# RWKV attention with a soft mixture of experts on one core: w, k and r laid channel-major by the host, decay scans over whole rows

## The chip, the core and the metric

The kernel runs on one core of a Trainium2 chip. The metric is the device time of one execution in microseconds (us). Of three runs of the kernel before, the fastest took 243.7, the slowest 246.23, and the median is 245.06 us. The traces come from a profiled execution of the same program. Engines are named as in the profile: PE (TensorE matmuls, PEld their weight loads), DVE (VectorE), ACT (ScalarE), POOL (GpSimd), SP (SyncE, which here only issues DMAs).

## The reference

Two parts follow each other. First a recurrent attention over B=4 batches, H=8 heads, S=768 tokens and D=48 channels, with a state matrix of 48x48 for each head that decays by w in every token:

```
for t in range(S):
    kt, vt, rt, wt = (k[:, :, t], v[:, :, t], r[:, :, t], w[:, :, t])
    cur = einsum('bhd,bhe->bhde', u[None] * kt, vt)
    y[:, :, t] = einsum('bhd,bhde->bhe', rt, state + cur)
    state = wt[:, :, :, None] * state + einsum('bhd,bhe->bhde', kt, vt)
```

Then x = y as 3072 tokens of 384 numbers goes through a soft mixture of 8 experts with 4 slots each: logits = x @ phi (32 columns), a softmax over all tokens gives what each slot takes in, each expert computes relu(slot @ w1) @ w2 with a hidden size of 1024, and a softmax over the 32 slots mixes the results into each token. The experts' weights are 25 MB, and all of it is float32.

## The kernel before

**Pairs and chunks.** The 32 combinations of batch and head are handled as 16 pairs of heads, and the 768 tokens of a pair as C=6 chunks of 128. In a pair's tiles the first head's 48 channels stand in rows 0 to 47 and the second's in rows 64 to 111, so these tiles have 112 rows; rows 48 to 63 are filler. For each chunk the recurrence is written as products: with G the decay from a token to the chunk's end and Rc the decay from the chunk's start divided by the decay of the whole chunk, K times G and R times Rc give the scores of every two tokens of a chunk by one matmul, and a state at each chunk's start is carried on by one short scan.

**One pass** of the loop over `it` (17 passes) works on two pairs at once, and on the logits of an older one:

- Stage A on pair `it`. w, k and r are loaded with tokens in rows. PE turns them, 128x112 at a time, with the identity as operand (`a_wT` L200, `a_turn` L235, 18 transposes). DVE scans w backward for G (`a_back` L212, one scan a chunk) and forward for Rc (`a_fwd` L221, one scan a chunk, out of PSUM both), and scales the turned k and r out of PSUM into `KTt` and `RTt` (`a_scale` L241). ACT copies the decays of whole chunks into `pat` and checks the range of the decays (`a_pat` L247, L249, `a_check` L205). POOL multiplies r, k and u (`d_rk` L254, `d_rku` L260) and DVE sums the product to `a` (`d_a` L265), the factor with which a token's own v enters.
- Stages B and C on pair `n = it-1`. PE turns five chunks of the scaled k back (`b_kn` L279, copied by ACT in L281), makes the scores in two halves of three chunks and two heads (`b_scores` L292; ACT copies two 128x384 tiles a half out of PSUM in L296 and POOL masks them in L297), and the 48x48 updates of the state (`b_u` L313). DVE scans the state over the chunks, a head at a time (`b_state` L321). PE then sums scores times v (`c_av` L335) and r times state (`c_inter` L348: one matmul with 112 rows for both heads, since `Sb` holds the two heads' states as a block diagonal), and DVE adds a·v (`av` is made by POOL, L270) and writes x, half a pair at a time (`c_evac` L357).
- In three of four passes from the fourth on (X), the logits of 128 columns of x: six transposes (`l_turn` L366, copied by ACT in L368), three matmuls with phi (`l_mm` L383), a copy (L388). In every fourth pass (Y: 6, 10, 14) the softmax of a finished batch, and in the pass behind it (Z: 7, 11) its slots.

**After the loop** come the rest of the softmax, the two projections of the experts (`hp` L515, `so` L549) and the mixing (`op` L593), with the output stored in 14 pieces.

**What sets the order.** The order is written by hand: each engine runs its instructions in the order of the program text, and waits at the head of its queue for what the next one needs. All loads and stores are issued by SP in that order too. The weights are loaded in thirds of a tile, `PER_IT[it]` thirds in a pass; what is left goes out after the loop.

## Time and profile before

| | us |
|---|---|
| runs: fastest, median, slowest | 243.7, 245.06, 246.23 |
| profiled execution: span | 244.0 |
| start, up to the first kn transposes of pass 3 | 34.55 |
| passes 3 to 15 | 147.70 |
| after that: pass 16, end of the softmax, experts, mixing | 61.75 |

The profiled execution's own time isn't listed apart from its span; the median of the runs lies 1.06 us above that span. The three stages are read from the chain of waits, in which every pass from the third on begins with the five transposes of L279.

In the rows of the prediction, the chain of waits gives start, duration and the engine, result and line of each piece of the chain that ended last. A group's row gives the line, engine, operation, result and source with their sizes, how often it ran, then its busy time in all, the mean duration of one in ns, and the idle time before it with what ended it. A timeline row begins with start and duration. The rows of stretches give the stretch, its length, the busy time of PE, PEld, DVE, ACT and POOL with the number of instructions, then the clock granted to PE as a share of full speed, the share of time for which the DMA engines were busy, and GB/s.

### The profile page before, as it was taken

The page shows a single profiled execution, that of the slowest core. Times are in us where ns is not written, and L with a number is a line of the kernel's source. Part 1 is how long each engine was busy: PE and PEld are TensorE (multiplying, and loading weights), DVE is VectorE, ACT ScalarE, POOL GpSimd, SP SyncE. Part 2 cuts the span into 40 slices and gives each one's busy share as a digit, 9 for nine tenths or more (in the row PEclk, how much of TensorE's full clock was granted, in tenths as well). Part 3 has the DMA queues.
Part 4 walks back from the last instruction along what each step waited for, and adds up shares of the span by engine and source line. Part 5 has one row for each costly group of instructions (what it writes and reads, how often), then busy time and mean ns, then how long its engine had stood idle before and what let it go on. Part 6 is the DMA issues. An engine that isn't in the chain of part 4 may idle for free.

```text
span 244.0 us, 7186 instructions
## 1 busy us (share of the span) xinstructions
PE 211.9 (87%) x2824; PEld 158.8 (65%) x2824; DVE 183.7 (75%) x464; ACT 97.2 (40%) x265; POOL 106.6 (44%) x156
## 2 busy tenths in 40 slices
PE   7759798989898899989798989897989999979850
PEld 3448586868677667768596768687768652346650
DVE  4997969798989888899979798999793744203540
ACT  0623436445262616372544354353536531203330
POOL 5346478465472828382737274563725131000000
PEclk9997979999997999999979999997999999999975
DMA  4988958939795969698696959994959278994994
GB/s 93 181 171 150 178 104 180 199 107 185 223 225 156 230 164 271 119 249 162 207 173 206 179 185 180 309 233 185 288 177 313 68 248 273 318 326 145 334 309 120
DMA packets 122072, 49.54 MB, mean 203 GB/s; under 512 B 101424, under 2 KB 118960, under 8 KB 122032
## 3 DMA queue, kind: packets, MB, share of 16 engines
q1 hardware_dynamic: 122032, 49.02, 79.2%
q8 instruction: 24, 0.39, 0.7%
q14 instruction: 16, 0.13, 0.2%
HBM read 44.29 MB, written 4.72 MB: 201 GB/s over the span
## 4 chain that ended last, share of the span: by engine, by line
PE 44%; DVE 38%; issue 6%; DMA 5%; SPq 2%; ACT 1%; POOL 1%; DVEq 0%; POOLq 0%; ACTq 0%
DVE Rc L221 13%; PE yp L348 13%; DVE G L212 12%; PE yp L335 6%; DVE Sb L321 6%; DVE KTt L241 5%; DMA wt<-in_moe_w_dram 4%; PE wt L200 4%; PE tp L279 4%; PE so L549 3%; PE hp L515 3%; PE op L593 3%; SPq L173 2%; PE sp L428 2%; PE tp L235 2%
## 5 line engine op out<-in xcount | busy, mean ns | idle before, releaser
L270 POOL TENSOR_TENSOR av<-vt,a 128x576 f32<-128x576 f32 x16 | 18.6, 1162 | 60.0 <-DVE x L357 38.9
L235 PE MATMUL tp<-ident,wrk 128*112 128x128 f32 x192 | 32.1, 299 | 13.8 <-DVE KTt L241 13.1
L212 DVE TENSOR_TENSOR_SCAN G<-wt,floor 112x128 f32<-112x128 f32 x96 | 32.0, 401 | 9.9 <-PE wt L200 9.6
L221 DVE TENSOR_TENSOR_SCAN Rc<-wt,Rc,ceil 112x127 f32<-112x127 f32 x96 | 37.6, 459 | 0.6
L348 PE MATMUL yp<-Sb,RTt 112*64 112x96 f32 x320 | 33.7, 353 | 3.8 <-DVE Sb L321 3.3
L235 PEld LDWEIGHTS tp<-ident,wrk 128*112 128x112 f32 x192 | 20.6, 140 | 24.2 <-DVE KTt L241 17.7
L297 POOL TENSOR_SCALAR_AFFINE_SELECT at<-at 128x384 f32<-128x384 f32 x64 | 31.8, 520 | 10.3 <-ACT at L296 10.2
L296 ACT COPY at<-ap 128x384 f32<-128x384 f32 x64 | 27.6, 482 | 20.6 <-PE ap L292 19.8
L281 ACT COPY kn<-tp 128x336 f32<-128x336 f32 (+1 forms) x32 | 11.0, 397 | 56.2 <-PE tp L279 56.2
L335 PEld LDWEIGHTS yp<-vt,at 128*64 128x64 f32 x768 | 29.0, 150 | 3.9 <-issue 1.6
L292 PE MATMUL ap<-RTt,KTt 48*128 48x128 f32 x384 | 30.9, 289 | 0.0
L335 PE MATMUL yp<-vt,at 128*64 128x48 f32 x768 | 30.8, 234 | 0.0
L292 PEld LDWEIGHTS ap<-RTt,KTt 48*128 48x128 f32 x384 | 24.8, 187 | 5.7 <-issue 4.7
L348 PEld LDWEIGHTS yp<-Sb,RTt 112*64 112x64 f32 x320 | 22.3, 157 | 7.2 <-DVE Sb L321 6.1
L254 POOL TENSOR_TENSOR rk<-wrk 128x576 f32<-128x576 f32 x16 | 22.6, 1414 | 9.4 <-ACT rk L205 8.7
L321 DVE TENSOR_TENSOR_SCAN Sb<-up,pat 48x288 f32<-48x288 f32 x32 | 24.0, 749 | 2.1 <-PE up L313 1.9
L260 POOL TENSOR_TENSOR rk<-rk,u_bc 128x576 f32<-128x576 f32 x16 | 22.5, 1405 | 1.9 <-DMA u_bc<-in_u_dram 1.7
L357 DVE TENSOR_TENSOR x<-yp,av 128x288 f32<-128x288 f32 x32 | 14.5, 454 | 7.8 <-PE yp L348 7.7
L241 DVE TENSOR_TENSOR RTt<-tp,Rc 112x384 f32<-112x384 f32 x32 | 16.5, 553 | 2.2 <-PE tp L235 1.8
L241 DVE TENSOR_TENSOR KTt<-tp,G 112x384 f32<-112x384 f32 x32 | 16.0, 538 | 0.0
L200 PE MATMUL wt<-ident,wrk 128*112 128x128 f32 x96 | 14.0, 282 | 1.3 <-POOL rk L254 0.7
L205 ACT ACTIVATE rk<-wrk,b_low 128x576 f32<-128x576 f32 x16 | 12.6, 786 | 6.5 <-DVE a L265 6.5
(125 smaller groups left out, 280.0 us busy)
## 6 DMA issues: line engine op xcount, KB each, us to landing
wt<-in_moe_w_dram SPq DMA_DIRECT2D x24, 512.0 KB, 4.9
wt<-in_moe_w_dram SPq DMA_DIRECT2D x4, 1536.0 KB, 6.9
vt<-in_v_dram SPq DMA_DIRECT2D x16, 288.0 KB, 4.0
wrk<-in_w_dram SPq DMA_DIRECT2D x30, 144.0 KB, 2.9
wrk<-in_k_dram SPq DMA_DIRECT2D x30, 144.0 KB, 3.4
wrk<-in_r_dram SPq DMA_DIRECT2D x30, 144.0 KB, 3.9
wt<-in_moe_w_dram SPq DMA_DIRECT2D x5, 576.0 KB, 8.2
wt<-in_moe_w_dram SPq DMA_DIRECT2D x3, 960.0 KB, 8.5
```

The costliest lines, as they stand in the source:

```text
L200: nc.tensor.transpose(out=wt[0:PITCH, c // 3, (c % 3) * P:(c % 3 + 1) * P], in_=win(st["t"], W_OFF, c), identity=ident)
L212: nc.vector.tensor_tensor_scan(out=G[0:PITCH, c, 0:P][:, ::-1], data0=wc[:, ::-1], data1=floor[0:PITCH].broadcast_to([PITCH, P]), initial= ...
L221: nc.vector.tensor_tensor_scan(out=Rc[0:PITCH, c, 1:P], data0=wc[:, 0:P - 1], data1=ceil[0:PITCH].broadcast_to([PITCH, P - 1]), initial=Rc ...
L235: nc.tensor.transpose(out=tp[0:PITCH, j, :], in_=win(st["t"], off, 3 * hf + j), identity=ident)
L241: nc.vector.tensor_tensor(out=st[which][0:PITCH, cs, :], in0=st[which, hf][0:PITCH], in1=fac[0:PITCH, cs, :], op=ALU.mult)
L254: nc.gpsimd.tensor_tensor(out=rk, in0=chd(st["t"], R_OFF), in1=chd(st["t"], K_OFF), op=ALU.mult)
L292: nc.tensor.matmul(out=aps[h][:, cc, :], lhsT=st["KT"][rows, c, :], rhs=st["RT"][rows, c, :], start=True, stop=True)
L296: nc.scalar.copy(out=at, in_=aps[h])
L297: nc.gpsimd.affine_select(out=at, in_=at, pattern=[[0, 3], [1, P]], compare_op=ALU.is_gt, fill=0.0, base=0, channel_multiplier=-1)
L321: nc.vector.tensor_tensor_scan(out=Sb[rows, h * D:(h + 1) * D, :].rearrange("p e n -> p (e n)"), data0=st["up"][rows].rearrange("p e n -> ...
L335: nc.tensor.matmul(out=yp[cols, cc, h, :], lhsT=st["AT", h, hf][:, cc, cols], rhs=st["vv"][:, h, 3 * hf + cc, :], start=first[th], stop=False)
L348: nc.tensor.matmul(out=st["yp", hf][cols, cc], lhsT=st["RT"][0:PITCH, c, cols], rhs=Sb[0:PITCH, :, c], start=False, stop=(cc == 2))
```

## The change

- The host hands over w, k and r of a pair as one array `wkr`: channels in rows, and in a row first 774 numbers of w (6 chunks of 128, with a 0 between them), then 768 of k and 768 of r. A pass loads it with two DMAs of 48 rows (`a_load`) into one of three rotating tiles `ld0`, `ld1`, `ld2`. v, phi, u, w1 and w2 are laid out by the host in the order of the tiles too, so that each row of a load is one piece; w2's columns are stored in the two parts (240 and 144) in which they are loaded at the end. The output is written as two arrays of 240 and 144 columns, which the host joins.
- The 18 transposes of w, k and r are gone. G is one backward scan over 774 numbers (`a_back` L177); the decay forward is one scan in place over w's own 774 (`a_fwd` L184), with the reciprocals of the chunks' decays put in at each chunk's start. k and r are scaled in place, each by one 112x768 multiplication (`a_scale` L190).
- `a` is made on PE: r times k, with channels in rows, is one POOL multiplication of 112x768 (`d_rk` L208), and six matmuls multiply it by u and sum over the channels (`d_a` L214), copied by ACT (L217). POOL's product with u and DVE's sum are gone.
- The state of both heads is one scan of 112x288 (`b_state` L264), no longer a block diagonal. r times state is therefore a matmul for each head (`c_inter` L293: 20 a pass with 48 rows, before 10 with 112).
- The result of a pair is one PSUM tile of two banks, evacuated by one instruction (`c_evac` L303).
- The order within a pass is another, the scores have three PSUM banks where they had two, and two thirds of a weight tile are loaded in each pass from 2 on.

The core of the diff:

```diff
+    def a_load(i, first=False):
+        t = lds[i % 3]
+        for lo, hi in ((0, K_OFF), (K_OFF, LOAD)) if first else ((0, LOAD),):
+            for h in range(2):
+                nc.sync.dma_start(out=t[64 * h:64 * h + D, lo:hi], in_=wkr[i, h, :, lo:hi])
...
+    def a_back(i):
+        t = lds[i % 3]
+        nc.vector.tensor_tensor_scan(
+            out=G[0:ROWS][:, ::-1], data0=t[0:ROWS, 1:SCAN + 1][:, ::-1], data1=g_base[0:ROWS][:, ::-1],
+            initial=1.0, op0=ALU.mult, op1=ALU.max)
+
+    def a_fwd(i):
+        t = lds[i % 3]
+        nc.vector.reciprocal(out=by_chunk(r_base)[:, :, 0], in_=by_chunk(G)[:, :, 0])
+        nc.vector.tensor_tensor_scan(
+            out=t[0:ROWS, 0:SCAN], data0=t[0:ROWS, 0:SCAN], data1=r_base[0:ROWS],
+            initial=1.0, op0=ALU.mult, op1=ALU.max)
+
+    def a_scale(i, off, fac, lo):
+        w_ = win(lds[i % 3], off)
+        nc.vector.tensor_tensor(out=w_, in0=w_, in1=by_chunk(fac)[:, :, lo:lo + P], op=ALU.mult)
...
     def d_a(i):
-        st = sts[i]
-        st["a"] = a = small.tile([P, C, 2, 1], F32, name="a")
-        nc.vector.tensor_reduce(out=a, in_=rk, axis=AX.X, op=ALU.add)
+        ap = ps_t.tile([P, C, 2], F32, name="aps", tag="tp")
+        for c in range(C):
+            nc.tensor.matmul(out=ap[:, c, :], lhsT=rk[0:ROWS, c * P:(c + 1) * P], rhs=u_sb[:, i % NG, :],
+                             start=True, stop=True)
+        sts[i]["a"] = a = small.tile([P, 2, C, 1], F32, name="a")
+        nc.scalar.copy(out=a.rearrange("p h c o -> p c (h o)"), in_=ap)
...
             for th in range(2):
                 cols = slice(64 * th, 64 * th + 64)
-                nc.tensor.matmul(
-                    out=st["yp", hf][cols, cc], lhsT=st["RT"][0:PITCH, c, cols], rhs=Sb[0:PITCH, :, c],
-                    start=False, stop=(cc == 2))
+                for h in range(2):
+                    rows = slice(64 * h, 64 * h + D)
+                    nc.tensor.matmul(
+                        out=st["y"][cols, h, c * D:(c + 1) * D],
+                        lhsT=t[rows, R_OFF + c * P + 64 * th:R_OFF + c * P + 64 * th + 64],
+                        rhs=Sb[rows, :, c], start=False, stop=(c == C - 1))
```

The order of a pass, as the program now has it (shortened to the attention and the logits):

```
        if B_:
            d_av(n)
        if A:
            a_back(it)
        if B_:
            b_kn(n)
            b_scores(n, 0)
        if A:
            d_a(it)
            a_scale(it, K_OFF, G, 1)
        if B_:
            b_u(n)
            b_state(n)
            b_scores(n, 1)
        if A:
            a_pat(it)
            a_fwd(it)
        if X:
            xT = l_turn(xb[mb], mg - 1, once, ps_t)
            ...
            l_part(mg - 1, xT, lts[mb], ps_t)
        if A:
            a_scale(it, R_OFF, lds[it % 3][:, 0:SCAN], 0)
        if B_:
            c_y(n)
            c_av(n, 0)
            c_inter(n, 0)
        ...
        if it + 1 < NIT:
            d_rk(it + 1)
            a_check(it + 1)
        if B_:
            c_av(n, 1)
            c_inter(n, 1)
            c_evac(n)
```

The PE queue in an X pass (pass 8), before: `wt` and `tp` from `wrk` are the transposes of w, k and r, `tp` from `x` those for the logits, `ap` the scores, `up` the state's updates, `lp` the logits, and `yp` the two products that sum to the attention's result.

```order
L279 MATMUL tp<-ident,KTt 128x112 x5
L200 MATMUL wt<-ident,wrk 112x128 x6
L366 MATMUL tp<-ident,x 128x128 x6
L292 MATMUL ap<-RTt,KTt 128x128 x6
L313 MATMUL up<-vt,kn 48x48 x10
L383 MATMUL lp<-xT,phi_sb 32x256 x3
L235 MATMUL tp<-ident,wrk 112x128 x6
L292 MATMUL ap<-RTt,KTt 128x128 x6
L235 MATMUL tp<-ident,wrk 112x128 x6
L335 MATMUL yp<-vt,at 64x48 x12
L348 MATMUL yp<-Sb,RTt 64x96 x4
L335 MATMUL yp<-vt,at 64x48 x12
```

Six matmuls of scores and ten of updates stood between the transposes of x and the logits made of them. The same pass on PE after, where `ld_101` is the pair's tile (k in the first place and r in the second of each score, k in the transposes) and `aps` the new product with u:

```order
L231 MATMUL tp<-ident,ld_101 128x112 x5
L242 MATMUL ap<-ld_101 128x128 x6
L214 MATMUL aps<-u_sb,rk 128x2 x6
L258 MATMUL up<-vt,kn 48x48 x10
L242 MATMUL ap<-ld_101 128x128 x6
L312 MATMUL tp<-ident,x 128x128 x6
L329 MATMUL lp<-xT,phi_sb 32x256 x3
L278 MATMUL y<-vt,at 64x48 x12
L293 MATMUL y<-Sb,ld_101 64x48 x8
L278 MATMUL y<-vt,at 64x48 x12
L293 MATMUL y<-Sb,ld_101 64x48 x12
```

The logits now stand directly behind the transposes that they need, and both halves of the scores ahead of them. The ACT queue of pass 8 before, where `kn`, `xT`, `at` and `lt` are copies out of PSUM, and L205 and L249 the checks:

```order
L281 COPY kn<-tp 128x336
L281 COPY kn<-tp 128x224
L205 ACTIVATE rk,chk<-wrk,b_low 128x576
L368 COPY xT<-tp 128x384 x2
L296 COPY at<-ap 128x384 x2
L388 COPY lt_1313<-lp 96x256
L296 COPY at<-ap 128x384 x2
```

The copies `xT` stood ahead of both pairs of score copies. The same queue after:

```order
L232 COPY kn<-tp 128x336
L232 COPY kn<-tp 128x224
L246 COPY at<-ap 128x384 x2
L217 COPY a<-aps 128x6x2
L246 COPY at<-ap 128x384 x2
L201 COPY pat_138<-G 112x48x5
L203 ACTIVATE junk_1232,chk<-G,b_one 112x6
L314 COPY xT<-tp 128x384 x2
L334 COPY lt_1093<-lp 96x256
L195 ACTIVATE xT,chk<-ld_100,b_low 112x768
```

The copies `xT` now stand behind both pairs of score copies, the copy of `a`, `pat` and one check.

More of the change, by code (lines that the diff above doesn't have):

```diff
@@ L75, in rwkv_soft_moe @@
     r32 = const.tile([P, NS], F32, name="r32")
[L76 to L77 removed]
     other = const.tile([TG, NTG, NS], F32, name="other")
[L79 to L83 removed]
+    u_sb = const.tile([ROWS, NG, 2], F32, name="u_sb")
     phi_sb = const.tile([P, KT, NS], F32, name="phi_sb")
@@ L225, in a_alloc @@
-    def a_alloc(i):
-        st = sts[i]
-        st["KT"] = kr.tile([P, C, P], F32, name="KTt")
-        st["RT"] = kr.tile([P, C, P], F32, name="RTt")
-    def a_turn(i, which, hf):
-        st = sts[i]
-        st[which, hf] = tp = ps_t.tile([P, 3, P], F32, name="tp")
-        off = K_OFF if which == "KT" else R_OFF
-        for j in range(3):
-            nc.tensor.transpose(out=tp[0:PITCH, j, :], in_=win(st["t"], off, 3 * hf + j), identity=ident)
-    def a_scale(i, which, hf):
-        st = sts[i]
-        fac = G[:, :, 1:P + 1] if which == "KT" else Rc
-        cs = slice(3 * hf, 3 * hf + 3)
-        nc.vector.tensor_tensor(out=st[which][0:PITCH, cs, :], in0=st[which, hf][0:PITCH],
-                                in1=fac[0:PITCH, cs, :], op=ALU.mult)
+        nc.sync.dma_start(out=vt, in_=v[i])
@@ L581, in mix @@
         wd = hi - lo
-        out_v = out.rearrange("(t p) d -> p t d", p=P)
+        out_v = (out_a, out_b)[half]
         sends, t = {}, 0
```

578 lines of the change are left out of this document (228 added, 350 removed).

## The prediction

> **What bounds the kernel now.** I read the chain of waits first, since engines with a high busy share can still be waiting for each other in turn. Pass 10 of the loop, and the marks of the stages:
>
> ```profile
> 6.64 2.37 DMA wrk<-in_r_dram
> ...
> 34.55 0.63 PE tp L279 x5
> ...
> 74.07 1.38 PE tp L235 x6
> ...
> 102.57 0.63 PE tp L279 x5
> 103.19 0.67 PE wt L200 x6
> 103.96 2.00 DVE G L212 x6
> 106.21 1.28 DVE Rc L221 x4
> 107.73 0.83 DVE Rc L221 x2
> 108.56 0.91 DVE KTt L241 x2
> 110.14 0.77 DVE Sb L321
> 110.96 0.89 PE yp L348 x8
> 111.84 0.69 PE yp L335 x24
> 112.53 1.03 PE yp L348 x12
> ...
> 182.25 0.63 PE tp L279 x5
> ...
> 207.81 9.86 DMA wt<-in_moe_w_dram
> ```
>
> A pass is a ring: PE turns k and w, DVE scans, scales and scans the state, PE finishes, and the next pass's transposes begin at 112.53+1.03=113.56, 11.0 us after 102.57. Some 6.4 us of it, from 103.96 to 110.91, is DVE work for which PE's last products wait. Neither engine is full, and both are on the path. Thirteen passes take 182.25-34.55=147.7 us (11.36 each, the passes with softmax work included); the start takes 34.55, the rest 244.0-182.25=61.75, of which 9.86 is a wait for the experts' weights.
>
> **The DVE half of the ring.** Groups of instructions by line, with the mean duration in ns of one:
>
> ```profile
> L212 DVE TENSOR_TENSOR_SCAN G<-wt,floor 112x128 f32<-112x128 f32 x96 | 32.0, 401 | 9.9 <-PE wt L200 9.6
> L321 DVE TENSOR_TENSOR_SCAN Sb<-up,pat 48x288 f32<-48x288 f32 x32 | 24.0, 749 | 2.1 <-PE up L313 1.9
> L241 DVE TENSOR_TENSOR RTt<-tp,Rc 112x384 f32<-112x384 f32 x32 | 16.5, 553 | 2.2 <-PE tp L235 1.8
> L270 POOL TENSOR_TENSOR av<-vt,a 128x576 f32<-128x576 f32 x16 | 18.6, 1162 | 60.0 <-DVE x L357 38.9
> L254 POOL TENSOR_TENSOR rk<-wrk 128x576 f32<-128x576 f32 x16 | 22.6, 1414 | 9.4 <-ACT rk L205 8.7
> L297 POOL TENSOR_SCALAR_AFFINE_SELECT at<-at 128x384 f32<-128x384 f32 x64 | 31.8, 520 | 10.3 <-ACT at L296 10.2
> ```
>
> A scan costs 401 ns for 128 and 749 for 288 numbers a row, so 2.2 ns a number and 0.12 us for itself: one over 774 is an estimated 1.8 us by that slope and 2.4 by L212's mean alone (401x774/128). I take 1.8, since the fixed part is paid once, and two are 3.6 where twelve now take 2.00+1.28+0.83 and gaps. K and R scaled in one piece of 768 each are at most twice 0.553, and with two fixed parts saved about 0.92. The state's two scans become one of 0.77. A DVE pass is then 1.8+0.92+0.77+0.2 (reciprocals)+1.8+0.92+0.75 (one eviction of 576, between 0.55 and 0.92 by L241) = 7.1 us, some 0.9 more on average for the softmax. No link to PE is left between these steps except the state scan, since no transpose feeds the scans and scalings any more. POOL loses the product with u: 1.16 (L270) + 4x0.52 + 1.9 (r times k, 1.41 taken from 576 to 768 numbers) = 5.1 us. Both are below what follows for PE, DVE even at 2.4 a scan.
>
> **The PE half.** The timeline of PE, then that of ACT, where the clock is full:
>
> ```profile
> 113.50 0.70 PE L279 MATMUL tp<-ident,KTt 112*128 112x112 f32 x5
> 114.03 0.82 PE L200 MATMUL wt<-ident,wrk 128*112 128x128 f32 x6
> 114.78 0.94 PE L292 MATMUL ap<-RTt,KTt 48*128 48x128 f32 x12
> 115.65 0.66 PE L313 MATMUL up<-vt,kn 128*48 128x48 f32 x20
> 116.24 0.87 PE L235 MATMUL tp<-ident,wrk 128*112 128x128 f32 x6
> 117.03 0.94 PE L292 MATMUL ap<-RTt,KTt 48*128 48x128 f32 x12
> ```
>
> ```profile
> 118.06 0.86 ACT L296 COPY at<-ap 128x384 f32<-128x384 f32 x2 [0.77 <-PE ap L292]
> 118.80 0.62 ACT L247 COPY pat<-G 112x240 f32<-112x240 f32 x1
> 119.32 0.31 ACT L249 ACTIVATE junk<-G,b_one 112x6 f32<-112x6 f32 x1
> 119.52 0.19 ACT L249 ACTIVATION_READ_ACCUMULATOR junk<-G,b_one 112x1 f32 x1
> ```
>
> Matmuls overlap at their ends, so I price them from start to start: kn 0.53, a half of scores 0.87 (115.65-114.78), the updates 0.59, six transposes 0.79. The change takes 18 transposes (3x0.79=2.4) from PE and adds two things that the trace does not show. The product with u is 12 matmul records (six, each in two parts) with 128-wide weights and two columns; by the 20 narrow records of L313 it would be 0.36, by the transposes at 0.13 each 1.58; I take 0.87, as for the scores, whose weight loads are alike. r times state becomes 40 records with 48 columns where it was 20 with 96: between 0.029 each as in L335 (0.69/24), so 1.17, and the 0.89+1.03=1.92 of today; I take 1.17, since records of L335 have the same columns and their price has not to do with rows. The X pass in PE's new order:
>
> - kn 0.53, scores 0.87, product with u 0.87, updates 0.59, scores 0.87: issued by 3.73. The transposes of x end at 4.52.
> - ACT can copy the second scores from 2.86+1.0=3.86 on (118.06-117.03=1.0 from their start to the copies). Behind them stand pat (0.74 after them), the check (0.52) and its accumulator, 0.39 together from 119.32 on, so the copies xT begin at 5.51, and with two copies of the L296 kind and a handover (0.92) the logits start at 6.43. All else on PE is queued behind them: it stands 1.9 us.
> - logits 0.56 (three matmuls with 256 columns, estimated between 0.39 and 0.79), scores times v 0.70 twice, r times state 1.17: 9.5 us.
>
> So PE has 7.6 us of work and waits 1.9 in ten of the thirteen passes; DVE with 7.1 to 8 fits in, with the eviction last and 2 us of room. Two more prices, the slots from the chain of waits and the softmax's exponential from the instructions of its tile:
>
> ```profile
> 88.28 1.42 PE sp L428 x12
> ```
>
> ```profile
> L410 ACT ACTIVATE dT<-lt,nM x1: 514/514/514, 116.5 to 116.5; 96x256 f32<-96x256 f32 x1
> ```
>
> A Y pass has no logits, but transposes of that exponential, which ACT gives out behind the same check: 5.51 plus 0.51 and 0.19 for its sum, 0.4 for four narrow transposes and 2.57 for the products, about 9.2. Passes 7 and 11 add the slots, 10.9. ACT has about 6.2 us of copies a pass, POOL 5.1: both hidden by PE's 9.5; if PE fell below 8, DVE would be late next. The sum: 8x9.5+3x9.2+2x10.9=125.4, against 147.7.
>
> **The clock.** The last price is of the 1.9 us wait. Three stretches, and PE's clock as granted in them:
>
> ```profile
> 50.38:53.79 3.41, 2.58 (x42) 2.01 (x42) 3.40 (x8) 1.67 (x5) 2.31 (x4) 1.00 0.05 17
> ...
> 70.86:74.27 3.41, 2.18 (x41) 1.76 (x40) 3.34 (x10) 1.91 (x7) 3.41 (x6) 1.00 0.98 314
> 74.27:77.69 3.42, 3.42 (x38) 3.06 (x36) 3.34 (x8) 0.64 (x2) 0.40 (x2) 0.50 0.34 79
> ```
>
> After 3.41 us in which PE was busy for 2.18, the next 3.42 us were granted half the clock; after 2.58 they weren't. So 0.9 to 1.2 us of idle time in such a window suffices. A wait of 1.9 us leaves that much in one window unless it is split near its middle: I count a drop in 9 of 10 passes. A drop showed as 1.38 for six transposes (74.07) where 0.79 is usual, so 3.4 us at half clock do the work of some 2.0. That costs 1.4 where PE is the bound throughout, and nothing where DVE is late anyway; I take 1.2, since after the wait PE has 3.1 us of work without another wait. Thirteen passes: 13x0.9x1.2=14, and the loop is 139.5, so 8.2 us less than before.
>
> The Trainium skill, in "TensorE: Matmul & The Clock Gate", section "HAM oscillation — how this bites in real kernels", puts the rule as PE gaps of over about 3.4 us. By it a wait of 1.9 would cost no clock and the loop would be 125.4. The rows differ: a window with 1.23 us idle in all was followed by half clock, so the sum goes by the rows, and the rule's result is rival B.
>
> **Start, end and loads.** The first pass now waits for eleven issues and a landing at 6.64+2.37=9.0; four DMAs of w, k and r come first in the new order, so scans start at an estimated 6.5 (4.5 to 7). Pass 0's scans and scalings, with POOL's 1.9 for r times k ahead of k's scaling, end near 12.2; pass 1 with PE at half clock near 20.4; pass 2 on DVE's bound of 7.7 near 28.1. That is 6.5 less than 34.55. The end keeps its matmuls. Its transfers get longer rows. The page's GB/s in 40 slices, and a stretch of the loop's end:
>
> ```profile
> GB/s 93 181 171 150 178 104 180 199 107 185 223 225 156 230 164 271 119 249 162 207 173 206 179 185 180 309 233 185 288 177 313 68 248 273 318 326 145 334 309 120
> ```
>
> ```profile
> 182.00:184.00 2.00, 1.00 1.06 397
> ```
>
> In the last weights' slices, of 6.1 us each, 318 and 326 GB/s were moved, in the output's 334 and 309; 397 was reached elsewhere. At 397 the wait of 9.86 would be 8.0 and the output's two slices 9.9 instead of 12.2, so the end gains between 0 and 4.2; I take 3, as these transfers are the end's bound. A pass loads 888 KB of w, k and r, 295 of v and 1,049 of weights, 5.6 us at 397 GB/s. They are asked for a pass ahead and hidden under 9.5; only under 235 GB/s (2,232 KB in 9.5 us) would they show.
>
> Sum: 244.0-8.2-6.5-3.0=226.3 us of span, 17.7 less; the median of the runs stood 1.06 above the profiled span, so I predict 227.
>
> **Rivals.**
>
> A, the forecast: PE's wait for xT and the drops of the clock that follow take back most of what the transposes were worth. 227 us.
>
> B, the wait costs no clock. For it: PE's work is denser in the rest of the pass than now. Against it: the rows above. It gives 227-14=213.
>
> C, DVE and POOL hold each other up. Both new scalings and both scans read two operands from SBUF, where today one comes from PSUM. In the softmax there is one pair of such instructions that overlap:
>
> ```profile
> L567 POOL COPY at<-cn x3: 343/347/667, 188.7 to 191.8; 128x192 f32<-128x192 f32 x3
> ...
> L568 DVE TENSOR_TENSOR at<-cn,vt x6: 347/355/520, 189.9 to 192.8; 128x192 f32<-128x192 f32 x6
> ```
>
> There the POOL copy took 667 ns instead of 347 and the DVE product 520 instead of 355. If each of the four DVE instructions waits for one POOL instruction (5.1 us in six, 0.85 each), DVE has 7.1+3.4+0.9=11.4 a pass, and becomes the bound with 13x11.4=148: no gain in the loop, 236 in all. The Trainium skill, in "SBUF — State Buffer", section "Who interferes with whom", says that a DVE instruction with two SBUF inputs and a GpSimd instruction that reads SBUF exclude each other. The pair above agrees as far as it goes; whether scans do so no row shows.
>
> D, slower: the clock stays at half. With a wait in each pass the window behind the drop might again be too idle, and so on. At 1.7 times its price PE's 7.6 us are 12.9, and with the wait 14.5 a pass: 13x14.5=188, 40 more than before, against 9.5 less at the two ends, 276. It decides once passes average over 12.1 (147.7+9.5 over 13), i.e. with half clock in over half of the time. Against it: in the trace a window at half clock is full of work (3.42 of 3.42 in 74.27) and the full clock is back in the next.
>
> E, no change: the loop is bound by something that the trace doesn't show (the 3.6 us of loads, 112-row scans from SBUF at a higher price, 3 us more), 240 to 247.
>
> **How the numbers follow.** The forecast gets 0.57, B 0.14, C 0.13, E 0.08, D 0.08. 227 is the likeliest case. Its own terms give: a drop at 0.5 to 1.4 each instead of 1.2 (-8 to +2), the product with u -6 to +9 over thirteen passes, r times state up to +10, the end -1 to +3. B's 213 with the ends' spread sets the lower bound at 208, and C's 236 with a part of the scans' price sets the upper one at 242; outside lie D, most of E, and a corner of B, together under 0.2. A measurement of this kernel can tell about 1% from no change. Faster by more than that (under 242.6): A, B and C, 0.84; within it, E, 0.08; slower, D, 0.08.
>
> **What the profile after would show.** Scans of 112x774 near 1.8 us and scalings near 0.92, or both longer where POOL is at work (C). On PE an idle stretch near 1.9 us ahead of the logits in each X pass, ended by ACT's copies xT, and a clock of 0.5 in one window of about each pass (A); a mean clock near 1.0 would be B, one below 0.7 in the loop D. Passes near 9.5 to 10.8 us, the third's kn transposes near 28, and an end near 59 after pass 15. I am wrong if the idle stretch is missing, if DVE is busy without a break, or if six matmuls with u take over 2 us.

## The result and the profile after

The changed kernel takes 297.98 us (median of four runs, 291.56 to 306.91), where the kernel before took 244.91 beside it. Two of the four runs (291.56 and 293.18) lie well below the other two (302.78 and 306.91) and carry the comparisons here, with a mean of 292.4. By them it is slower by a ratio of 1.194, 95% interval 1.186 to 1.202; 227 was predicted, and 208 to 242 given as the range. The profiled execution took 291.56 us, with a span of 289.9 against 244.0.

Three stretches of the kernel after, up to the kn transposes of pass 3, passes 3 to 15, and the rest (columns as in the rows of stretches shown before):

```profile
0.00:43.14 43.14, 31.35 (x320) 26.07 (x321) 25.24 (x29) 12.71 (x33) 23.45 (x27) 0.59 0.71 139
43.14:227.88 184.74, 164.75 (x2095) 138.43 (x2095) 121.43 (x125) 71.64 (x201) 105.48 (x77) 0.63 0.62 151
227.88:289.90 62.02, 50.82 (x636) 31.27 (x635) 22.13 (x57) 18.32 (x47) 7.41 (x14) 0.90 0.68 256
```

and the loop of the kernel before:

```profile
34.55:182.25 147.70, 134.84 (x1912) 107.87 (x1913) 133.27 (x336) 67.63 (x190) 80.18 (x102) 0.97 0.81 199
```

The start is 8.6 us longer than before (43.14 against 34.55), the loop 37.0 (184.74 against 147.70), the end 0.3 (62.02 against 61.75). In the loop DVE is busy for 121 us where it was 133, as the change meant it to be. PE is busy for 165 where it was 135, although 18 transposes a pass are gone: the clock granted to it is 0.63, where it was 0.97.

The page says the same, with engines' busy time, the clock in 40 slices, and the shares of the chain that ended last:

```profile
PE 246.9 (85%) x3047; PEld 195.8 (68%) x3047; DVE 168.8 (58%) x211; ACT 102.7 (35%) x281; POOL 136.3 (47%) x118
...
PEclk9555555995555556955965588555556999799985
...
PE 77%; ACT 9%; DMA 4%; issue 3%; POOL 2%; SPq 1%; DVE 1%; POOLq 0%; ACTq 0%; DVEq 0%
```

The same shares before:

```profile
PE 44%; DVE 38%; issue 6%; DMA 5%; SPq 2%; ACT 1%; POOL 1%; DVEq 0%; POOLq 0%; ACTq 0%
```

DVE had 38% of the chain and now has 1. The ring between PE and DVE is broken as forecast, and PE carries the chain almost alone, at half clock in most slices of the loop. One such pass in the chain of waits:

```profile
182.64 1.12 PE tp L231 x5
183.77 1.58 PE ap L242 x12
185.35 2.65 PE aps L214 x12
188.00 0.98 PE up L258 x20
188.97 1.63 PE ap L242 x12
...
192.31 0.76 ACT xT L314 x2
193.11 1.08 PE lp L329 x6
194.19 1.45 PE y L278 x24
195.64 0.61 PE y L293 x16
196.25 1.45 PE y L278 x24
197.70 0.82 PE y L293 x24
198.52 1.12 PE tp L231 x5
```

It takes 15.9 us, with one wait of PE (about 1.1 us ahead of the logits). The same pieces at full clock, in the timeline of PE for the part of pass 4 before its clock drops:

```profile
56.99 0.70 PE L231 MATMUL tp<-ident,ld 112*128 112x112 f32 x5
57.62 0.94 PE L242 MATMUL ap<-ld 48*128 48x128 f32 x12
58.49 1.50 PE L214 MATMUL aps<-u_sb,rk 112*128 112x2 f32 x12
59.92 0.66 PE L258 MATMUL up<-vt,kn 128*48 128x48 f32 x20
60.51 0.94 PE L242 MATMUL ap<-ld 48*128 48x128 f32 x12
61.38 0.87 PE L312 MATMUL tp<-ident,x 128*128 128x128 f32 x6
63.99 0.63 PE L329 MATMUL lp<-xT,phi_sb 128*32 128x256 f32 x6 [1.74 <-ACT xT L314]
```

Here is the wait of the forecast, 1.74 us where 1.9 was expected, ended by the copies xT. From 56.99 to the logits' end it is 7.6 us where the forecast had 7.0; the product with u, 1.43 from start to start, is the one piece that was priced far too low (0.87). So at full clock the forecast holds to within a microsecond for this part of a pass. It is the clock that doesn't come back.

Three windows of 3.41 us of the kernel after, each with the clock granted in it:

```profile
62.34:65.75 3.41, 1.76 (x46) 1.29 (x46) 3.38 (x3) 2.67 (x8) 3.18 (x3) 1.00 0.94 241
86.23:89.64 3.41, 3.41 (x24) 3.17 (x24) 2.11 (x2) 1.02 (x3) 3.07 (x3) 0.50 1.06 172
154.50:157.91 3.41, 3.41 (x22) 2.91 (x21) 3.31 (x3) 1.58 (x4) 2.92 (x2) 0.50 0.98 168
```

The first, with 1.65 us of idle time, is followed by half clock, as in the kernel before. The other two are without a gap on PE, and half clock goes on behind both. In the kernel before, a full window at half clock was the end of it (74.27 to 77.69). What differs is what PE does: the window at 86.23 holds 24 matmul records in place of 38, and half of them are the product with u, each of which loads 128-wide weights and moves two columns; these twelve take 2.72 of the 3.41 us.

### The profile page after: what moved, and what is told of

Same layout as the page of the kernel before. It is cut to its first block, busy times and chain, and to the rows that moved or that the text cites. A ratio compares the mean times of both kernels' runs of the same rounds, so it can differ in the third digit from the quotient of the medians.

```text
span 289.9 us, 7255 instructions
## 1 busy us (share of the span) xinstructions
PE 246.9 (85%) x3047; PEld 195.8 (68%) x3047; DVE 168.8 (58%) x211; ACT 102.7 (35%) x281; POOL 136.3 (47%) x118
## 4 chain that ended last, share of the span: by engine, by line
PE 77%; ACT 9%; DMA 4%; issue 3%; POOL 2%; SPq 1%; DVE 1%; POOLq 0%; ACTq 0%; DVEq 0%
PE ap L242 15%; PE y L278 13%; PE aps L214 12%; PE y L293 7%; PE tp L231 5%; PE up L258 5%; PE hp L461 4%; PE so L496 4%; DMA ld<-in_pad_dram 4%; PE lp L329 3%; ACT xT L314 3%; PE op L540 3%; ACT at L246 2%; PE sp L374 2%; PE tp L312 2%
## 5 line engine op out<-in xcount | busy, mean ns | idle before, releaser
L247 POOL TENSOR_SCALAR_AFFINE_SELECT at<-at 128x384 f32<-128x384 f32 x64 | 59.9, 961 | 36.9 <-ACT at L246 36.9
L214 PE MATMUL aps<-u_sb,rk 112*128 112x2 f32 x192 | 38.6, 329 | 9.7 <-POOL rk L208 9.7
L214 PEld LDWEIGHTS aps<-u_sb,rk 112*128 112x128 f32 x192 | 37.2, 295 | 13.2 <-POOL rk L208 10.5
L242 PE MATMUL ap<-ld 48*128 48x128 f32 x384 | 45.9, 396 | 0.2 <-DVE ld L190 0.2
L278 PEld LDWEIGHTS y<-vt,at 128*64 128x64 f32 x768 | 37.3, 193 | 10.9 <-POOL at L247 5.4
L278 PE MATMUL y<-vt,at 128*64 128x48 f32 x768 | 42.3, 281 | 0.6 <-POOL at L247 0.6
L242 PEld LDWEIGHTS ap<-ld 48*128 48x128 f32 x384 | 37.5, 280 | 5.3 <-DVE x L303 2.8
L208 POOL TENSOR_TENSOR rk<-ld 112x768 f32<-112x768 f32 x16 | 33.1, 2068 | 12.8 <-DMA ld<-in_pad_dram 10.8
L177 DVE TENSOR_TENSOR_SCAN G<-ld,g_base 112x774 f32<-112x774 f32 x16 | 28.2, 1760 | 6.3 <-DMA ld<-in_pad_dram 6.3
L303 DVE TENSOR_TENSOR x<-y,av 128x576 f32<-128x576 f32 x16 | 12.1, 758 | 32.6 <-PE y L293 32.5
L184 DVE TENSOR_TENSOR_SCAN ld<-ld,r_base 112x774 f32<-112x774 f32 x16 | 29.6, 1852 | 1.6
L190 DVE TENSOR_TENSOR ld<-ld,G 112x768 f32<-112x768 f32 x16 | 26.0, 1626 | 4.7 <-POOL rk L208 3.3
L264 DVE TENSOR_TENSOR_SCAN Sb<-up,pat 112x288 f32<-112x288 f32 x16 | 12.0, 753 | 23.0 <-PE up L258 23.0
L293 PE MATMUL y<-Sb,ld 48*64 48x48 f32 x640 | 23.6, 292 | 0.0
L293 PEld LDWEIGHTS y<-Sb,ld 48*64 48x64 f32 x640 | 18.1, 189 | 2.5
L190 DVE TENSOR_TENSOR ld<-ld 112x768 f32<-112x768 f32 x16 | 17.3, 1083 | 0.5
L231 PE MATMUL tp<-ident,ld 112*128 112x112 f32 x80 | 16.6, 361 | 0.0
```

Source lines behind the costliest of these rows:

```text
L177: nc.vector.tensor_tensor_scan(out=G[0:ROWS][:, ::-1], data0=t[0:ROWS, 1:SCAN + 1][:, ::-1], data1=g_base[0:ROWS][:, ::-1], initial=1.0, o ...
L184: nc.vector.tensor_tensor_scan(out=t[0:ROWS, 0:SCAN], data0=t[0:ROWS, 0:SCAN], data1=r_base[0:ROWS], initial=1.0, op0=ALU.mult, op1=ALU.max)
L190: nc.vector.tensor_tensor(out=w_, in0=w_, in1=by_chunk(fac)[:, :, lo:lo + P], op=ALU.mult)
L208: nc.gpsimd.tensor_tensor(out=rk[0:ROWS], in0=t[0:ROWS, R_OFF:R_OFF + S], in1=t[0:ROWS, K_OFF:K_OFF + S], op=ALU.mult)
L214: nc.tensor.matmul(out=ap[:, c, :], lhsT=rk[0:ROWS, c * P:(c + 1) * P], rhs=u_sb[:, i % NG, :], start=True, stop=True)
L231: nc.tensor.transpose(out=tp[:, c - lo, 0:ROWS], in_=kv[:, c, :], identity=ident[0:ROWS, 0:ROWS])
```

## The experiments

Three theories. **W**: the clock goes by the work that the array does in a window of 3.41 us (columns moved, times the share of the array in use), at full and at half clock alike; a pass of the changed kernel has 4,660 such columns where one before had 7,140 (counted from the matmul records of the loops), and at half clock too few of them fall into a window to leave it. **I**: it goes by the idle time of PE, as the prediction had it. **S**: PE only follows DVE and POOL, which shut each other out of SBUF (rival C of the prediction).

### Filling the wait with work, and with records that do none

```diff
+    def fill_pe(i):
+        for _ in range(N_FILL):
+            nc.tensor.matmul(out=sts[i]["y"][:, 0, 288:512], lhsT=zb[:, 0:P], rhs=zb[:, 0:224],
+                             start=True, stop=True)
...
             xT = l_turn(xb[mb], mg - 1, once, ps_t)
+        if B_:
+            fill_pe(n)
```

> Added to the changed kernel: 20 bf16 matmuls of zeros (128x128 weights, 224 columns) on PE between the transposes of x and the logits in every pass from the second on, into an unused part of the result's PSUM bank; nothing left out. Theory W (the clock follows the work that the array does in a stretch of 3.41 us, columns times the share of the array in use; records that only load weights count for nothing): each pass gets 4,480 columns of full-array work beside the some 4,700 it has, the granted clock in the loop rises from 0.6 to over 0.9, and in spite of the added 1.9 us of PE a pass is 10 to 11 us; total 240 to 255. Theory I (the clock follows the idle time of PE's queue): the same, since the wait is filled. Theory S (DVE and POOL lock each other out, and PE only follows): the clock may rise, but passes stay near 14 us; total 290 to 310.

The second kernel differs in the matmul, and has 8 of them where the first has 20:

```diff
-            nc.tensor.matmul(out=sts[i]["y"][:, 0, 288:512], lhsT=zb[:, 0:P], rhs=zb[:, 0:224],
+            nc.tensor.matmul(out=sts[i]["y"][:, 0, 288:290], lhsT=ident, rhs=ident[:, 0:2],
```

> Added to the changed kernel at the same place as the dense filling: 8 float32 matmuls with 128x128 weights and 2 columns (16 records, 1.9 us at full clock by the 1.43 us of the 12 records of L214, 3.5 at half); nothing left out. Theory W: they occupy PE but do no work on the array, so the clock stays near 0.6 in the loop and the time is 298 plus up to 13 times the 1.8 us by which they outlast the wait, 295 to 325. Theory I: PE isn't idle, so the clock is back above 0.9 as with the dense filling, 240 to 255.

Measured: 267.37 us with the dense filling (263.71 and 271.02), 339.59 with the thin one (338.3 and 340.88). Both loops, from the kn transposes of pass 3 to those of pass 16. First the dense one:

```profile
40.98:199.59 158.61, 157.41 (x2355) 132.78 (x2355) 120.68 (x125) 70.78 (x201) 110.79 (x78) 0.86 0.73 179
```

and the thin one:

```profile
49.26:273.21 223.95, 223.95 (x2303) 197.34 (x2303) 114.92 (x125) 71.48 (x201) 103.73 (x77) 0.72 0.51 125
```

In the thin one PE is busy for 223.95 of 223.95 us. The mean of 0.72 is too high, since this trace's clock records begin only at 136 us and what is ahead of them counts as full; the durations tell the clock. In its timeline of PE, late in the loop:

```profile
241.43 2.72 PE L215 MATMUL aps<-u_sb,rk 112*128 112x2 f32 x12
...
246.63 3.57 PE L274 MATMUL y<-ident 128*128 128x2 f32 x16
```

the product with u takes 2.72 us, as at half clock in the kernel after, and the filling 3.57. In the dense one:

```profile
165.67 1.50 PE L215 MATMUL aps<-u_sb,rk 112*128 112x2 f32 x12
...
169.27 2.08 PE L274 MATMUL y<-zb 128*128 128x224 bf16 x20
171.28 0.63 PE L335 MATMUL lp<-xT,phi_sb 128*32 128x256 f32 x6
```

Here the same product takes 1.50. Two microseconds of PE a pass were added, and the kernel became some 29 us faster (263.71 against 292.4). Theory I falls: with PE busy throughout, the thin kernel is at half clock for 123 of the 137 us of its loop for which the clock is on record, where theory I had full clock and 240 to 255 us. The clock can also fall while PE has no gap. Two windows of the dense kernel, one behind the other:

```profile
42.03:45.45 3.42, 3.42 (x54) 3.11 (x52) 3.31 (x3) 1.21 (x5) 3.42 (x2) 1.00 1.08 202
45.45:48.86 3.41, 3.41 (x19) 2.87 (x19) 3.27 (x4) 2.42 (x7) 3.17 (x4) 0.50 0.94 164
```

The first holds 1,277 columns of work, counted as theory W does. The two fillings differ in type too, bf16 and float32, but float32 as such doesn't hold the clock down: the loop of the kernel before is float32 and had 0.97. W's direction holds in both, with a size that was off: dense filling was to give 240 to 255, but half clock still came back in several passes, and the thin one cost more than the upper 325.

### Taking POOL away

```diff
     def d_rk(i):
         t = lds[i % 3]
+        if i:
+            return
         nc.gpsimd.tensor_tensor(out=rk[0:ROWS], in0=t[0:ROWS, R_OFF:R_OFF + S], in1=t[0:ROWS, K_OFF:K_OFF + S],
...
-            nc.gpsimd.affine_select(
-                out=at, in_=at, pattern=[[0, 3], [1, P]], compare_op=ALU.is_gt,
-                fill=0.0, base=0, channel_multiplier=-1)
```

> Left out: POOL's multiplication r times k, its a times v and its masking of the scores in all passes but the first one's products (outputs differ), so that DVE and POOL meet nowhere in the loop. Theory S: DVE's scalings go back to 0.92 us from 1.63 and 1.08, the loop's passes to below 10.5 us, total 225 to 245. Theories W and I: DVE's scalings shorten as well, but the 77% of the chain that lie on PE stay at half clock; total 275 to 300.

Measured: 300.19 us (300.07 and 300.32), no faster than the changed kernel, where S had 225 to 245. The groups of DVE's scans and scalings in the kernel after:

```profile
L208 POOL TENSOR_TENSOR rk<-ld 112x768 f32<-112x768 f32 x16 | 33.1, 2068 | 12.8 <-DMA ld<-in_pad_dram 10.8
L177 DVE TENSOR_TENSOR_SCAN G<-ld,g_base 112x774 f32<-112x774 f32 x16 | 28.2, 1760 | 6.3 <-DMA ld<-in_pad_dram 6.3
...
L190 DVE TENSOR_TENSOR ld<-ld,G 112x768 f32<-112x768 f32 x16 | 26.0, 1626 | 4.7 <-POOL rk L208 3.3
...
L190 DVE TENSOR_TENSOR ld<-ld 112x768 f32<-112x768 f32 x16 | 17.3, 1083 | 0.5
```

and without POOL:

```profile
L191 DVE TENSOR_TENSOR ld<-ld,G 112x768 f32<-112x768 f32 x16 | 15.3, 958 | 2.2 <-POOL rk L211 1.6
L191 DVE TENSOR_TENSOR ld<-ld 112x768 f32<-112x768 f32 x16 | 15.3, 958 | 0.5
```

So the two do hold each other up, k's scaling by 0.67 us, and it costs the changed kernel nothing, since PE is what it waits for. S falls as the cause.

### The product with u

Left out, and alternatively made cheap:

```diff
     def d_a(i):
+        if i:
+            sts[i]["a"] = a_fix
+            return
```

> Left out: the six matmuls with u and their copy on ACT in all passes but the first, whose a is used throughout (outputs differ). Theory W: the 1.4 us (2.65 at half clock) in which PE does next to nothing goes, work per window rises above the limit for much of the time, the clock in the loop is above 0.8 and the time falls by 40 or more, to 230 to 255. Theory I: they were busy time, so the clock isn't better than 0.68 and only their own 13 to 16 times 2.65 us go: 255 to 265.

```diff
-    rk = decay.tile([P, S], F32, name="rk")
+    rk = decay.tile([P, S], BF16, name="rk")
+    u16 = fixed.tile([ROWS, NG, 2], BF16, name="u16")
...
-            nc.tensor.matmul(out=ap[:, c, :], lhsT=rk[0:ROWS, c * P:(c + 1) * P], rhs=u_sb[:, i % NG, :],
+            nc.tensor.matmul(out=ap[:, c, :], lhsT=rk[0:ROWS, c * P:(c + 1) * P], rhs=u16[:, i % NG, :],
```

> The changed kernel with the bf16 product with u alone, in the changed kernel's own order. The product falls to 0.3 to 0.5 us a pass from 1.43 (2.65 at half clock). Theory W: a pass at half clock of 13 us has 1,200 columns a window, too few to leave half clock, so only the product's own time goes: 258 to 270, clock of the loop near that of no_aps. If the product were the cause of the half clock by itself: full clock, 225 to 240.

Measured: 267.86 us without it (266.78 and 268.94), 274.26 with the bf16 product (274.65 and 273.86). Against 292.4, some 18 to 25 us go, which is not more than the product's own 2.65 us in 12 to 16 passes would give (32 to 42); PE still takes half clock in most of the loop (a mean clock of 0.58 there without the product). So it isn't the product by itself that holds the clock down. For W both were misses, the second by 4 us; in the first, theory I's 255 to 265 came nearer than W's 230 to 255: a pass at half clock without the product takes about 13.2 us, and 4,660 columns in it are 1,200 in 3.41 us, still too few. That number, which the expectation for the bf16 product then used, could have been worked out for the first.

### The order of the pass, and the two together

In `reorder` both halves of the scores and the updates stand directly behind kn, and the logits behind the first products:

```diff
         if B_:
+            c_y(n)
             b_kn(n)
             b_scores(n, 0)
+            b_u(n)
+            b_scores(n, 1)
         if A:
             d_a(it)
             a_scale(it, K_OFF, G, 1)
+        if X:
+            xT = l_turn(xb[mb], mg - 1, once, ps_t)
         if B_:
-            b_u(n)
             b_state(n)
-            b_scores(n, 1)
...
             c_av(n, 0)
             c_inter(n, 0)
+        if X:
...
+            l_part(mg - 1, xT, lts[mb], ps_t)
```

> The changed kernel with its passes in another order alone: both halves of the scores and the updates directly behind kn, the product with u behind them, ACT's copies xT ahead of pat and the check, the logits behind the first half of the products; nothing left out. PE's wait ahead of the logits goes. Theory W (the clock follows the array's work in a window of 3.41 us, and half clock holds itself, since at half clock a pass of 14.7 us has only some 4,700x3.41/14.7=1,090 columns of full-array work a window where about 1,450 are needed): the loop is entered at half clock and stays there for most of it; passes near 14, total 270 to 290. Theory I (idle time of PE): with no wait left the clock is full, passes near 9, total 225 to 240.

> The order of reorder, with r times k written as bf16 by POOL and u as bf16, so that the product with u is six records with bf16 weights instead of twelve. If its time is the loading of weights, it falls from 1.43 us (2.65 at half clock) to 0.4 to 0.7. Theory W: 12.8 us a pass at half clock, some 1,250 columns a window, still under the limit for most of the loop, total 250 to 275. Theory I: full clock, 215 to 230.

> The order of reorder, with bf16 matmuls of zeros added on PE: 44 instead of 9 before the first pass (128x128 weights, 512 columns), 16 of 224 columns in each of passes 1 and 2, and 4 of 224 columns behind the product with u in every pass; nothing left out. Theory W: the loop is entered at full clock and the 896 columns a pass keep it there: 4,700+896 in 9.3 us are 2,050 a window; passes of 9 to 10 us, total 222 to 240. Theory I: as for reorder, plus 0.4 us a pass.

> reorder_fill and reorder_bf together; nothing left out. Theory W: full clock in the loop, passes of 8.5 to 9.5 us, then bound by DVE with POOL (8.0 us of DVE with the time in which the two exclude each other); total 215 to 232. Theory I: the same as reorder_bf, plus 0.4 a pass.

Measured: 264.66 with the order alone, 257.04 with the bf16 product too, 257.5 with the order and some filling, 242.72 with all three (two runs each; 246.02 before). The order gives 28 us, more than W expected and much less than theory I did: removing the wait shortens a pass at full clock and so raises the work in a window, but the kernel is still at half clock in long stretches. The part of its loop for which the clock is on record:

```profile
81.30:201.21 119.91, 114.33 (x1665) 94.33 (x1660) 99.75 (x103) 57.37 (x159) 84.99 (x59) 0.74 0.72 176
```

PE is busy for 95% of it, and at half clock for half of it. Each of the three measures is worth 7 to 28 us, and none is enough alone. The two versions with filling were slower than W had them (222 to 240 and 215 to 232), and theory I's ranges were missed by all four. In the bf16 product the group's row of `reorder_bf`

```profile
L217 PE MATMUL aps<-u,rk 112*128 112x2 bf16 x96 | 5.1, 168 | 7.8 <-POOL rk L211 7.8
```

shows six records a pass (96 in 16 passes) where there were twelve.

### More filling, a warm start, and POOL's share

```diff
-N_WARM = 9
+N_WARM = 44
+N_FILL = 6
+N_EARLY = 16
...
         if A:
             d_a(it)
+        if B_:
+            fill_pe(n, N_FILL)
...
+            fill_pe(n, N_EARLY if it < 3 else N_FILL)
             c_av(n, 0)
```

> As reorder_fill_bf, but with 12 instead of 4 zero matmuls a pass from pass 3 on (6 behind the product with u, 6 ahead of the first products), 1.1 us of PE at full clock and 2,690 columns; nothing left out. Theory W: about 7,400 columns in a pass of 10 us are 2,500 a window, like the kernel before; half clock in fewer than 40 of the loop's some 140 us where it was 82, and the loop is then bound by DVE and POOL; total 228 to 238. Theory I: no better than reorder_fill_bf, as the added matmuls stand where PE isn't idle; 243 to 255.

> The changed kernel with 44 instead of 9 zero matmuls ahead of the first pass, so that the passes begin at full clock. Theory W: at full clock a pass of 10.7 us has 1,500 columns a window, just at the limit; the clock drops in one of the first X passes and then stays down as before; only the start gets shorter, 285 to 297. If half clock holds only since it was entered at half: 230 to 250.

For the next, `b_scores` masks its second half on DVE:

```diff
+            if hf:
+                nc.vector.tensor_tensor(out=at, in0=aps[h], in1=upper, op=ALU.mult)
+                continue
             nc.scalar.copy(out=at, in_=aps[h])
```

> As fill12_bf, and the second half of the scores is masked by DVE on its way out of PSUM (times a triangle of ones) instead of copied by ACT and masked by POOL; the state's scan goes ahead of it. With the clock held, what is left would be DVE and POOL shutting each other out (some 5.4 us of DVE and 5.1 of POOL a pass); here POOL has 4.0 and DVE 1.1 more outside of it. If that bounds the passes: 1 us less a pass than fill12_bf, 215 to 228. If it doesn't: the same as fill12_bf or slower by DVE's 1.1.

Measured: 242.6 us for `fill12_bf` (240.61 to 244.24 but for one of ten runs, 261.68), a ratio of 0.991 to the kernel before, interval 0.985 to 0.996: about 1%, too little to count as a gain here. W had 228 to 238. The tripled filling did to the clock what W said, 27 us of half clock in the loop where fewer than 40 were expected. But the total is no better than the 242.72 of `reorder_fill_bf`, as theory I had it, so something else bounds it. The loop now takes 138.4 us, for which 139.5 were forecast for the change, and 147.7 were needed before; the start (37.45) and the end (63.08) are 2.9 and 1.3 us longer than before. Its passes at full clock are as short as forecast for the change; kn transposes in its chain of waits:

```profile
37.45 0.45 PE tp L234 x3
...
46.59 0.63 PE tp L234 x5
...
55.73 0.63 PE tp L234 x5
```

9.1 us each. In other passes there is a new wait. Its timeline of POOL, and then of DVE, in a later pass:

```profile
101.59 1.16 POOL L225 TENSOR_TENSOR av<-vt,a 128x576 f32<-128x576 f32 x1
102.70 1.00 POOL L250 TENSOR_SCALAR_AFFINE_SELECT at<-at 128x384 f32<-128x384 f32 x2
103.86 2.97 POOL L250 TENSOR_SCALAR_AFFINE_SELECT at<-at 128x384 f32<-128x384 f32 x2 [0.16 <-ACT at L249]
```

```profile
101.11 4.20 DVE L180 TENSOR_TENSOR_SCAN G<-ld,g_base 112x774 f32<-112x774 f32 x1
105.42 1.02 DVE L193 TENSOR_TENSOR ld<-ld,G 112x768 f32<-112x768 f32 x1
```

The scan, 1.76 us on average in the kernel after, takes 4.20 while POOL is at work, and the two maskings that begin at 103.86, during the scan, take 2.97 where the two ahead of them took 1.00. With the clock mended, rival C's mechanism comes into play; how much of the total it costs wasn't measured. The version with half of the maskings on DVE was to gain a microsecond a pass by it and didn't: 249.0 us (245.17 to 252.52), where 215 to 228 were expected if it did. In its page POOL waits 35 us for the loads of w, k and r in all, where `fill12_bf` had 11, so loads that arrive late may be another bound there. Which of the two would come first in a better version is left open.

`after_warm` took 306.77 us (305.53 and 308.0), at the upper end of the changed kernel's four runs or above it, where W had 285 to 297. Its passes 2 to 5 begin at the same times as those of the changed kernel to 0.02 us (30.36, 43.14, 57.05, 68.20): the zero matmuls held the clock for the first stretch only and it was at half before the kn transposes of pass 2. It doesn't tell what an entry at full clock would do.

### Work and clock over all traces

For 928 windows of 3.41 us in the fourteen traces (all windows whose clock the records give, on the grid of the records), the matmul records were counted by the window in which they start, each with its columns times its rows and columns of the array over 128x128. The last column counts the windows followed by full clock:

```
clock in the window   work in the window      windows   next at full
full                  under 1,200             34        0
full                  1,200 to 1,600          84        46
full                  over 1,600              395       384
half                  under 1,200             206       0
half                  1,200 to 1,600          161       31
half                  over 1,600              48        38
clock in the window   PE busy in the window   windows   next at full
half                  under 2.30 us           50        0
half                  2.30 to 3.35 us         65        2
half                  over 3.35 us            300       67
```

The best single limit by work (1,424) is wrong for 60 of 928 windows, the best by PE's busy time for 325, and the best by busy time multiplied with the clock in the window for 119. Of 300 windows at half clock in which PE has no gap to speak of, 233 are followed by half clock; in 16 windows at full clock PE has no gap either, and half clock follows: they hold 1,174 to 1,469 columns. These limits were chosen on the windows that they are judged by. The 1,450 that the expectation for `reorder` named before the last eight versions ran is wrong for 49 of their some 510 windows. By columns alone, whatever the share of the array, 79 of all are wrong, and without the transposes 140, so which measure of the work the chip takes isn't settled, and between 1,200 and 1,600 columns the count doesn't decide.

As a forecast of a kernel's time W did badly all the same: of its eleven totals only the one for `reorder_bf` was met (257.04 in 250 to 275), and four more were missed by under 6 us. Where theory I had a total of its own it was missed each time, by 0.4 us in `fill12_bf`, by 3 without the product, and by more in the others. What the runs show of W is what follows a window; how often a kernel that stands near the limit falls and gets back couldn't be forecast from it.

## Why the prediction was wrong, step by step

- **What bounds the kernel, and the DVE half: right.** The ring is gone, DVE's share of the chain fell from 38 to 1%, the scans took 1.76 where 1.8 was said, and k's and r's scalings 0.96 without POOL where 0.92 was said. With POOL at work they took 1.63 and 1.08, and DVE was busy for 9.3 us a pass (121.43/13) where 8.0 with the softmax was said; that cost nothing, since DVE has only 1% of the chain.
- **PE's wait ahead of the logits: right** in place and size (1.74 for 1.9, ended by the copies xT).
- **The product with u: mis-sized.** The sum took 0.87, and it is 1.43 at full clock and 2.65 at half. The range ran to 1.58. The scores were the wrong row to take, though their weights are 128 wide as well: in both kernels' traces their twelve records come in six pairs, one record of each head, which start 0.007 us apart, with some 0.11 us to the next pair, while the twelve of the product start 0.11 us apart one by one, like the transposes. r times state was 1.15 (0.49 and 0.66) where 1.17 was said.
- **The clock: the step that failed.** The prediction saw that a wait of 1.9 us costs the clock, and let each drop last one window: "in the trace a window at half clock is full of work (3.42 of 3.42 in 74.27) and the full clock is back in the next", it said against rival D. It took busy time as the measure. That row's window held 1,528 columns of work, the one at 86.23 after the change 225, both with PE busy throughout. The change removed a third of the array's work in a pass (7,140 to 4,660 columns) and put in, with the product with u, time of PE with next to no work of the array; the prediction read the removal as pure gain. With the table above the sum can be made: at full clock 4,660 columns in 10.5 us are 1,510 in a window, at the edge; at half clock, in 15.5 us, 1,025, and none of the 206 windows under 1,200 at half clock got back. So the term that failed is the 1.2 us for a drop, 14 us in all: the loop was 45.2 us over the forecast.
- **Rival D: it came about**, in its consequence: half clock in most of the loop, at 14.2 us a pass (184.74/13) where 14.5 was worked out (its own terms, 7.6x1.7 and 1.9, make 14.8). Its reason was only half right. The windows behind a drop have too little work for the array; PE's queue needn't be idle in them. It got a chance of 0.08.
- **Rival B** (no price for the clock) fell with it, and with it the Trainium skill's rule as read there ("TensorE: Matmul & The Clock Gate", section "HAM oscillation — how this bites in real kernels", gaps of over some 3.4 us): here PE's longest wait in the loop was 2.3 us, and yet PE was at half clock for 135 of its 185 us, in windows without any gap too.
- **Rival C: there, but not the cause.** POOL's and DVE's instructions do exclude each other, and scans do so too, which the prediction left open; taking POOL away changed nothing (300.19). The Trainium skill's sentence in "SBUF — State Buffer", section "Who interferes with whom", agrees with the runs: a scan with two SBUF inputs took 4.20 us beside POOL where it usually took 1.76.
- **The start: wrong by 15 us** (43.14, forecast 28.1). Loads and POOL, from the chain of waits of the kernel after:

```profile
5.00 11.61 DMA ld<-in_pad_dram
16.85 3.32 POOL rk L208
20.21 2.72 PE aps L214 x12
```

  The filler rows of the second tile, issued at 5.00 behind that tile's w, k and r, land at 16.6, and POOL's product behind them takes 3.32 where 1.8 is usual, with DVE's scan of the same tile, 1.77 from 16.79 on, beside it. The forecast had the first scan at 6.5 (it began at 9.19) and did not count the filler loads, which are new. Passes 1 and 2 then ran at half clock; pass 2 took 12.8 us (30.36 to 43.14) where 7.7 was counted.
- **The end: wrong by 3 us.** Longer rows brought nothing in sum, 62.02 for 61.75. The wait of 9.86 us for the experts' weights is gone from the chain, but it wasn't the end's bound: PE is busy for 50.82 us there, before for 50.10, and now carries that part of the chain.

Two small slips of the prediction change nothing: rival E's 3.6 us of loads are 5.6 in the paragraph on loads, and the DVE work between 103.96 and 110.91 is 6.2 us by the chain, not 6.4. The sum that was off: start +15.0, loop +45.2 (184.74 for 139.5), end +3.3, 63.5 in all, which is 289.9 less the predicted span of 226.3 to within rounding.

## What to carry to other kernels

Before work is taken off PE, count how much the array does in a window of the clock's length, here 3.41 us, in columns and not in busy time, both before and after: a kernel that waits as long but works less can lose its clock, and then at half clock has even less work in a window. Here some 1,400 columns were the limit. Matmuls with wide weights and two columns cost PE its time and give the clock nothing; a product of that kind is better made in bf16 (0.32 us a pass here, 5.1/16) or elsewhere. Where an engine's wait can't be removed, dense matmuls in it can pay for themselves, as 2 us a pass of them made this kernel some 29 us faster, though still slower than before the change.

## What the runs showed of the hardware

- A PE that is busy for 223.95 of 223.95 us stayed at half clock (123 of the 137 us on record) with float32 matmuls of two columns among its work, and was at full clock in most of the loop (114 of 159 us) when the same gap was filled with 20 bf16 matmuls of 224 columns.
- But for the last of a trace, the clock's records last 3.41 us or a multiple of it, and no window under 1,200 columns (240 of them, at either clock) was followed by full clock.
- A record of the float32 product with u took 0.12 us at full clock (1.43/12) and 0.22 at half.
- Scans with two operands in SBUF and POOL instructions hold each other up by about a whole instruction: a scan that usually takes 1.76 us took 4.20, and a POOL product of 1.8 us took 3.32 beside a scan of 1.77.
- In some traces the clock's records begin late, and the mean granted clock then reads too high: 0.79 over the whole run for the kernel with the thin filling, whose records begin at 136 us and whose matmuls took their half-clock times.
